# Attention in steps of half a unit: TensorE's work sorted by kinds, eight transposes in two banks, other lags

## The chip, the cores and the metric

The kernel runs on one core of a Trainium2 chip. The metric is the device time of one execution in microseconds (us), as the median of several runs. Five engines work side by side, each on its own queue, in the order of the program: TensorE (PE: matrix products and transposes; its weight loads are listed apart as PEld), VectorE (DVE), ScalarE (ACT), GpSimd (POOL) and SyncE (SP, which issues DMAs). Matrix results land in PSUM, in banks of 512 float32 columns; everything else lives in SBUF.

## The reference

Causal attention for 2 batches of 12 heads, 448 positions and 64 numbers per head, then two feed-forward parts on the 896 tokens, the first with a product of two projections, the second with a SiLU. All inputs are float32.

```
scores = where(mask, -1e9, (q @ k^T) / 8);  attn = softmax(scores);  x = attn @ v
x is laid out as 896 tokens x 768
y = ((x @ w_a) * (x @ w_b)) @ w_out          # w_a, w_b 768 x 1536, w_out 1536 x 768
h = y @ w_in                                 # 768 x 2048
out = (h * sigmoid(h)) @ w2_out              # 2048 x 768
```

## The kernel before

Attention works on 12 units (u) of two heads each; the first six belong to batch 0. The 448 queries of a unit are seven blocks j of 64, and block j meets only the 64*(j+1) keys that the mask leaves. GROUPS deals the blocks out to four slots, so that each slot's scores fill one PSUM bank: (6), (5, 0), (4, 1), (3, 2). One slot of the program holds, in this order on TensorE:

- the scores of a group. A block j >= 3 is multiplied as "halves" (a high and a low part of q and k in a faster float format; three matmuls, L565), a smaller block in plain float32 (one matmul per head, L569). In the trace and in the order's rows these are `sc<-kh,qh` and `sc<-k,q`.
- LAG_PV = 11 slots later the product with v (`xo<-ptr,v`, L627, float32), by blocks of 128 keys: one block in each of a unit's first two slots, two in the third, none in the fourth;
- LAG_T = 5 slots later the transposes of the group's softmax rows (`pt<-ident,p`, L610), four of 128x128 into one PSUM bank. The bank is emptied into `ptr` in SBUF one slot later (L710): by ACT, for block 4 by DVE. There are two such banks, and until slot 32 a third, which is later needed for other work.

Between scores and transposes lies the softmax: DVE adds the mask and takes the extreme of each row (soft, L577), ACT takes the exponential (L581), DVE inverts the rows' sums (normalize, L590 and L591), POOL multiplies the rows by that (L594). Normalize comes twice per unit, each for two groups. POOL also makes the high half of the next unit's q and k (`qh`, `kh`, L538), DVE the low half (`ql`, `kl`, L543). When all four blocks of keys are done, finish copies the unit's result out of PSUM: ACT as `xh` (L383) and `xf` (L385), DVE as `xl` (L389).

The order of the program is written out by the loop over slots: what a slot defers goes to a list (late) with a slot and a priority, and is issued from it in the order of the priorities. Beside attention, the first weights of the dense part are converted from 64-bit words (convert): on DVE L225, L230 and L256, on ACT L213, L219 and L252. A timeline places these, in units of seven matmuls per slot.

Once the scores are through, the loop runs on for the slots in which the lagging transposes and products still come (here called the drain). These are filled with the first products of the dense part, which need batch 0 alone (early_products, `acc`, L295): 12 pieces of three matmuls. Behind the attention come some 450 us of dense products on TensorE.

Of the kernel before, what the change touches and what calls it, by code (L numbers as in the profile page):

```python
# [10 lines left out]
F32 = mybir.dt.float32  # L11
# [19 lines left out]
CONV2 = 52  # L31
WARM = 8
BIG = 3
NQ = 3
SLOT_HI = 0
SLOT_LO = 2
SUMS0 = 44
SUMS_MM = 3
SPARE = 6
# [10 lines left out]
SLOT_MM = 7  # L50
# [12 lines left out]
def fused_kernel(ctx: ExitStack, tc: tile.TileContext, qk, v, w_ab, w_mid, w_in, w_out, out):  # L63
# [33 lines left out]
    ps_g = [ctx.enter_context(tc.tile_pool(name=f"ps_g{i}", bufs=1, space=PSUM)) for i in range(2)]  # L97
# [85 lines left out]
    line = Timeline()  # L183
# [267 lines left out]
    sums_x = Sums()  # L451

    granules = []
# [23 lines left out]
    with tc.manual_schedule():  # L477

        with ExitStack() as actx:
# [6 lines left out]
            sm_p = sctx.enter_context(right(name="sm_p", bufs=3))  # L486
# [24 lines left out]
            nblk = [j // 2 + 1 for j in range(NJ)]  # L511
            p_sb = [[p_p.tile([P, P * nblk[j]], F32, name=f"p{s}_{j}") for j in range(NJ)] for s in range(2)]
            U = [dict() for _ in range(NU)]
            late, now = {}, [0]
            n_slots = NU * len(GROUPS) + LAG_PV + 2
            NS = len(GROUPS)

            def defer(k, prio, fn):
                late.setdefault(now[0] + k, []).append((prio, fn))
# [21 lines left out]
            def halves_lo(u):  # L541
                for n, src, _ in sources(u):
                    nc.vector.tensor_tensor(  # L543
                        out=U[u][n + "l"], in0=src, in1=U[u][n + "h"].bitcast(F32), op=ALU.subtract)

# [1 line left out]
                U[u]["v"] = v_p.tile([P, NKB, P], F32, tag="v", name="v")  # L547
                nc.sync.dma_start(out=U[u]["v"], in_=v[u])

            def scores(u, i):  # L550

                t = U[u]
                if i == 0:
                    for n in ("sums", "nmax", "rcp"):
                        t[n] = st_p.tile([P, NJ], F32, tag=n, name=n)
                bank = ps_s.tile([P, 512], F32, tag="s", name="sc")
                sm = sm_p.tile([P, S], F32, tag="sm", name="sm")
                o = 0
                for j in GROUPS[i]:
                    K = D * (j + 1)  # L560
                    sc = bank[:, o:o + K]
                    o += K
                    if "qh" in t and j >= BIG:
                        for n, (a, k) in enumerate((("qh", "kh"), ("qh", "kl"), ("ql", "kh"))):
                            nc.tensor.matmul(out=sc, lhsT=t[a][:, j - BIG].rearrange("p h q -> p (h q)"), rhs=t[k][:, 0:K],  # L565
                                             start=(n == 0), stop=(n == 2))
                    else:
                        for h in range(2):
                            nc.tensor.matmul(  # L569
                                out=sc[h * D:(h + 1) * D], lhsT=q_sb[u % NQ][:, h, j * D:(j + 1) * D],  # L570
                                rhs=t["k"][:, 0:K], start=True, stop=True,
                            )
                    defer(0, 2, partial(soft, u, j, sc, sm[:, o - K:o], K, COL[j]))

            def soft(u, j, sc, sm, K, c):
                t = U[u]
# [20 lines left out]
                    )  # L597

            def transposes(u, i):
                t = U[u]  # L600
                if i == 0:
                    t["pt"] = pt_p.tile([P, NKB, 2, S], F32, tag="ptr", name="ptr")
                pool, tag = (ps_g[1], "g") if now[0] < b0_done - 4 and now[0] % 3 == 0 else (ps_t, "t")
                bank = pool.tile([P, NKB, 2, D], F32, tag=tag, name="pt")
                o = 0
                for j in GROUPS[i]:
                    pt = bank[:, o:o + nblk[j]]
                    o += nblk[j]
                    for kb in range(nblk[j]):
                        nc.tensor.transpose(  # L610
                            out=pt[:, kb].rearrange("p h q -> p (h q)"),
                            in_=p_sb[u % 2][j][:, kb * P:(kb + 1) * P], identity=ident,
                        )
                    copy = nc.vector.tensor_copy if j in EVAC_DVE else nc.scalar.copy
                    dst = t["pt"][:, 0:nblk[j], :, j * D:(j + 1) * D]
                    defer(1, 1, partial(copy, out=dst, in_=pt))

            def pv(u, kb):
                t = U[u]
                b, chunk = divmod(u, NP)  # L620
                if kb == 0:
                    pool, tag = ps_x, "x"
                    if u % 2:
                        pool, tag = ps_g[0], "g"
                    t["x"] = pool.tile([P, 512], F32, tag=tag, name="xo")
                for h in range(2):
                    nc.tensor.matmul(  # L627
                        out=t["x"][h * D:(h + 1) * D, kb * P:S], lhsT=t["v"][:, kb, h * D:(h + 1) * D],
                        rhs=t["pt"][:, kb, h, kb * P:S], start=(kb == 0), stop=(kb == NKB - 1),
                    )  # L630
                if kb == NKB - 1:
                    defer(1, 0, partial(finish, b, chunk, t["x"][:, 0:S]))

            tasks = []

# [26 lines left out]
            line.now = -n_slots * SLOT_MM  # L662
            line.convert(granules[0], (CONV0 - n_slots) * SLOT_MM, (CONV1 - CONV0) * SLOT_MM)
            line.convert(granules[1], (CONV1 + 1 - n_slots) * SLOT_MM, (CONV2 - CONV1) * SLOT_MM)
# [12 lines left out]
            b0_done = (NP - 1) * NS + LAG_PV + NKB + 1  # L677
            fill, n_fill = early_products(), 2 * NP
            done_fill = 0
            fill0 = NU * NS + 2  # L680
            for s in range(n_slots):
                now[0] = s
                if s == NU * NS + 1:
# [5 lines left out]
                u, i = divmod(s, NS)  # L689
                if i == 0 and 0 < u and u + 2 < NU:  # L690
                    load_qk(u + 2)
                if i == SLOT_HI and u + 1 < NU:
                    halves_hi(u + 1)
                if i == SLOT_LO and u + 1 < NU:
                    halves_lo(u + 1)
                if i == 0 and 0 < u <= NU:
                    load_v(u - 1)
                for what, lag in ORDER:
                    u, i = divmod(s - lag, NS)
                    if not 0 <= u < NU:  # L700
                        continue
                    if what == "scores":
                        scores(u, i)
                    elif what == "transposes":
                        transposes(u, i)
                    else:
                        for kb in PV[i]:
                            pv(u, kb)
                for _, fn in sorted(late.pop(s, ()), key=lambda e: e[0]):
                    fn()  # L710
                while tasks:
                    tasks.pop(0)()
                u, i = divmod(s - LAG_N, NS)
                if 0 <= u < NU and i % 2 == 1:
                    normalize(u, (i - 1, i))
                if s >= SUMS0:
                    sums_x.step()
                line.to((s + 1 - n_slots) * SLOT_MM)
                want = n_fill * max(0, s + 1 - fill0) // (n_slots - 3 - fill0)
                while done_fill < min(want, n_fill):  # L720
                    next(fill, None)
                    done_fill += 1
            run(fill)
            for fn in sorted(late):
                for _, f in late[fn]:
# [250 lines left out]
```

## Time and profile before

| | us |
|---|---|
| median of 3 runs (571.66 to 571.90) | 571.85 |
| the profiled execution, its own time | 571.69 |
| its span in the trace | 569.9 |
| TensorE busy in the span | 559.3 |
| DVE busy | 421.8 |
| ACT busy | 380.5 |
| POOL busy | 72.2 |

The span is what the trace covers; the time of an execution is 1.8 us more. Busy times are sums over the whole span. Attention fills roughly the first 107 us, so its part is read from stretches of that part alone, and a unit in steady state is one stretch that ends where the fourth group's transposes start the next unit.

### The profile page before, as it was taken

To read this page: it belongs to the slowest core of one execution; us is meant where nothing else is said; L and a number is where in the kernel's file an instruction comes from. 1 tells how busy PE (TensorE), PEld (TensorE's weight loads), DVE (VectorE), ACT (ScalarE), POOL (GpSimd) and SP (SyncE) were. 2 spreads that over 40 slices of the span, in tenths; PEclk is the share of its full clock that TensorE was granted. 3 is DMA by queue.
4 is the path that set the end of the run, shared out by engine and by line. 5 is a ranking of instruction groups with operands and counts; after the bars stand their busy time and mean duration, and the time that the engine had idled before them with its cause. 6 is when DMAs were issued, how large, how long until landed. Compare 5 with 4: busy or idle time off the path is not lost.

```text
span 569.9 us, 8400 instructions
## 1 busy us (share of the span) xinstructions
PE 559.3 (98%) x2978; PEld 490.4 (86%) x2978; DVE 421.8 (74%) x794; ACT 380.5 (67%) x754; POOL 72.2 (13%) x127
## 2 busy tenths in 40 slices
PE   8999997999999999999999999999999999999997
PEld 6666664799999999999999999999999999999996
DVE  6798887587989898969875688978887798342500
ACT  4989988674766666668745475888786996532601
POOL 6887764000000000000000000000000000000000
PEclk9999999999999999999999999999999999999999
DMA  7355323032333434333333333333324233541501
GB/s 246 116 178 139 121 65 141 1 112 110 112 110 112 136 134 161 117 118 109 114 110 112 110 112 110 112 113 110 112 96 143 75 113 111 165 142 54 176 0 64
DMA packets 18233, 65.41 MB, mean 115 GB/s; under 512 B 2192, under 2 KB 6928, under 8 KB 18192
## 3 DMA queue, kind: packets, MB, share of 16 engines
q1 hardware_dynamic: 18048, 64.77, 33.6%
q8 instruction: 23, 0.38, 0.3%
q14 instruction: 18, 0.15, 0.1%
q10 hardware_dynamic: 144, 0.11, 0.1%
HBM read 62.13 MB, written 2.75 MB: 114 GB/s over the span
## 4 chain that ended last, share of the span: by engine, by line
PE 93%; DVE 2%; ACT 2%; POOL 1%; issue 1%; DMA 1%; SPq 0%; POOLq 0%; DVEq 0%; ACTq 0%
PE acc L295 82%; PE pt L610 4%; PE xo L627 3%; PE sc L565 3%; PE sc L569 2%; DVE sm L577 1%; POOL p L594 1%; ACT ptr L710 1%; DMA k<-qk 1%; DVE wq L230 0%; ACT xf L385 0%; ACT p L581 0%; ACT xh L383 0%; DVE kl L543 0%; DVE ql L543 0%
## 5 line engine op out<-in xcount | busy, mean ns | idle before, releaser
L225 DVE SCALAR_TENSOR_TENSOR wq<-wr 128x768 uint32<-128x768 uint32 (+1 forms) x76 | 66.5, 877 | 28.4 <-ACT wr L219 27.7
L318 ACT COPY s<-acc 128x448 f32<-128x448 f32 x72 | 38.4, 533 | 63.1 <-PE acc L295 62.7
L219 ACT ACTIVATE wr<-wr,wbias 128x768 uint32<-128x768 uint32 (+1 forms) x76 | 69.9, 920 | 0.0
L213 ACT ACTIVATE wr<-wr 128x768 f32<-128x768 f32 (+1 forms) x76 | 63.8, 840 | 5.4 <-DMA wr<-w_out 4.0
L230 DVE SCALAR_TENSOR_TENSOR wq<-wr,wq 128x768 uint32<-128x768 uint32 (+1 forms) x76 | 64.0, 873 | 0.1
L594 POOL TENSOR_SCALAR p<-p,rcp 128x448 f32<-128x448 f32 (+6 forms) x84 | 56.3, 685 | 21.3 <-ACT p L581 15.6
L581 ACT ACTIVATE p<-sm,nmax 128x448 f32<-128x448 f32 (+6 forms) x84 | 43.0, 523 | 10.5 <-DVE nmax L577 9.5
L295 PE MATMUL acc<-th,wgbl 128*128 128x448 f32 x168 | 49.5, 366 | 0.0
L295 PE MATMUL acc<-th,wgbh 128*128 128x448 f32 x168 | 49.4, 366 | 0.0
L295 PE MATMUL acc<-th,wgal 128*128 128x448 f32 x168 | 49.4, 365 | 0.0
L295 PE MATMUL acc<-tl,wgah 128*128 128x448 f32 x168 | 49.4, 366 | 0.0
L295 PE MATMUL acc<-tl,wgbh 128*128 128x448 f32 x168 | 49.4, 365 | 0.0
L295 PE MATMUL acc<-th,wgah 128*128 128x448 f32 x168 | 49.3, 365 | 0.0
L610 PEld LDWEIGHTS pt<-ident,p 128*128 128x128 f32 x192 | 20.2, 141 | 22.4 <-issue 10.8
L610 PE MATMUL pt<-ident,p 128*128 128x128 f32 x192 | 31.0, 285 | 5.5 <-ACT ptr L710 4.4
L577 DVE CUSTOM_DVE_ANT_0 sm<-sc,mask 128x448 f32<-128x448 f32 (+6 forms) x84 | 31.9, 411 | 4.8 <-PE sc L569 4.8
L295 PEld LDWEIGHTS acc<-th,wgbh 128*128 128x128 f32 x168 | 31.5, 188 | 2.9 <-DVE s L767 0.2
L295 PEld LDWEIGHTS acc<-th,wgah 128*128 128x128 f32 x168 | 31.5, 188 | 2.7
L295 PEld LDWEIGHTS acc<-tl,wgah 128*128 128x128 f32 x168 | 31.6, 188 | 2.6
L295 PEld LDWEIGHTS acc<-th,wgal 128*128 128x128 f32 x168 | 31.5, 188 | 2.5
L295 PEld LDWEIGHTS acc<-th,wgbl 128*128 128x128 f32 x168 | 31.5, 188 | 2.5
L295 PEld LDWEIGHTS acc<-tl,wgbh 128*128 128x128 f32 x168 | 31.5, 188 | 2.5
(167 smaller groups left out, 1384.2 us busy)
## 6 DMA issues: line engine op xcount, KB each, us to landing
wr<-w_ab SPq DMA_DIRECT2D x24, 768.0 KB, 4.9
wr<-w_in SPq DMA_DIRECT2D x16, 768.0 KB, 4.5
wr<-w_out SPq DMA_DIRECT2D x24, 512.0 KB, 4.4
wr<-w_mid SPq DMA_DIRECT2D x12, 768.0 KB, 4.6
v<-v SPq DMA_DIRECT2D x12, 256.0 KB, 4.2
q<-qk SPq DMA_DIRECT2D x24, 112.0 KB, 2.8
k<-qk SPq DMA_DIRECT2D x12, 224.0 KB, 3.3
out<-o SPq DMA_DIRECT2D x11, 224.0 KB, 5.4
```

What stands on the lines that cost most here:

```text
L213: nc.scalar.activation(out=word(i, 1).bitcast(F32), in_=word(i, 1).bitcast(F32), func=AF.Copy, scale=2.0 ** -112)
L219: nc.scalar.activation(out=word(i, 0), in_=word(i, 0), func=AF.Relu, bias=wbias, scale=2.0 ** -29)
L225: nc.vector.scalar_tensor_tensor(out=xi(i), in0=word(i, 1), scalar=3, in1=word(i, 0), op0=ALU.logical_shift_left, op1=ALU.bitwise_or)
L230: nc.vector.scalar_tensor_tensor(out=xi(i), in0=word(i, 1), scalar=0x80000000, in1=xi(i), op0=ALU.bitwise_and, op1=ALU.bitwise_or)
L295: nc.tensor.matmul(out=acc[:, 0:S], lhsT=w, rhs=a, start=first, stop=last, skip_group_check=True)
L318: nc.scalar.copy(out=t, in_=acc[:, 0:S])
L565: nc.tensor.matmul(out=sc, lhsT=t[a][:, j - BIG].rearrange("p h q -> p (h q)"), rhs=t[k][:, 0:K], start=(n == 0), stop=(n == 2))
L577: nc.vector.tensor_tensor_reduce(out=sm, in0=sc, in1=mask[:, S - K:S], op0=ALU.add, op1=ALU.min, scale=-(D ** -0.5), scalar=3.0e38, accum_ ...
L581: nc.scalar.activation(out=p_sb[u % 2][j][:, 0:K], in_=sm, func=AF.Exp, bias=t["nmax"][:, c:c + 1], scale=-1.0, accum_out=t["sums"][:, c:c ...
L594: nc.gpsimd.tensor_scalar(out=pj, in0=pj, scalar1=t["rcp"][:, COL[j]:COL[j] + 1], scalar2=1.0, op0=ALU.mult, op1=ALU.mult,)
L610: nc.tensor.transpose(out=pt[:, kb].rearrange("p h q -> p (h q)"), in_=p_sb[u % 2][j][:, kb * P:(kb + 1) * P], identity=ident,)
L627: nc.tensor.matmul(out=t["x"][h * D:(h + 1) * D, kb * P:S], lhsT=t["v"][:, kb, h * D:(h + 1) * D], rhs=t["pt"][:, kb, h, kb * P:S], start= ...
```

## The change

The loop now counts steps of half a unit, two groups each. In a step TensorE gets first all halves products of both groups, then their float32 scores, then the product with v for two blocks of keys (LAG_PV = 5 steps), then eight transposes (LAG_T = 2 steps). The eight transposes go into two banks, and the table COPIES says which block lies where and who empties it: in a unit's first half one bank by a single ACT copy of 512 columns, the other by three copies on DVE; in the second half one bank by an ACT copy of 512, the other by ACT copies of 384 and 128. For that, most transposes write their 128 columns as two runs of 64. The third bank serves every third bank while u < 8. The deferred work of a step is sorted differently: ACT's copies, then finish, then the low halves and all softs of the step, then DVE's copies and normalize. The 12 early pieces come in four steps from step 24 on, at the start of each.

```diff
-PV = ((0,), (1,), (2, 3), ())
-EVAC_DVE = (4,)
-LAG_N = 1
-LAG_T = 5
-LAG_PV = 11
-ORDER = (("scores", 0), ("pv", LAG_PV), ("transposes", LAG_T))
+COPIES = (
+    ((0, "scalar", 0, 2, 5, 2), (1, "vector", 2, 1, 5, 2), (1, "vector", 3, 1, 6, 1), (1, "vector", 0, 1, 0, 1)),
+    ((0, "scalar", 0, 1, 1, 4), (1, "scalar", 1, 1, 2, 3), (1, "scalar", 2, 1, 4, 1)),
+)
+LAG_T = 2
+LAG_PV = 5
+FILL_STEPS = 4
...
-            def scores(u, i):
+            def scores(u, groups):
...
+                for n, j, sc in sorted(work, key=lambda e: e[1] < BIG):
                     K = D * (j + 1)
...
-                    defer(0, 2, partial(soft, u, j, sc, sm[:, o - K:o], K, COL[j]))
+                if groups[0] and u + 1 < NU:
+                    defer(0, 2, partial(halves_lo, u + 1))
+                for n in range(len(groups)):
+                    defer(0, 2, partial(soft_group, u, [(j, sc) for m, j, sc in work if m == n]))
...
-                pool, tag = (ps_g[1], "g") if now[0] < b0_done - 4 and now[0] % 3 == 0 else (ps_t, "t")
-                bank = pool.tile([P, NKB, 2, D], F32, tag=tag, name="pt")
...
+                bank = []
+                for _ in range(2):
+                    pool, tag = (ps_g[1], "g") if n_banks[0] % 3 == 2 and u < NP + 2 else (ps_t, "t")
+                    n_banks[0] += 1
+                    bank.append(pool.tile([P, 512], F32, tag=tag, name="pt"))
+                place, o = {}, [0, 0]
+                for n, copy, kb, nkb, j, nj in COPIES[i]:
+                    size = nkb * nj * 2 * D
+                    src = bank[n][:, o[n]:o[n] + size].rearrange("p (k h q) -> p k h q", k=nkb, h=2)
...
+                            place[j + c, kb + a] = src[:, a, :, c * D:(c + 1) * D]
...
+                    if copy == "vector":
+                        defer(1, 3, partial(nc.vector.tensor_copy, out=dst, in_=src))
+                    else:
+                        defer(1, 0, partial(nc.scalar.copy, out=dst, in_=src))
...
+            for d in range(n_steps):
...
+                while done_fill < min(n_fill * max(0, d + 1 - 2 * NU) // FILL_STEPS, n_fill):
+                    next(fill, None)
+                    done_fill += 1
+                if u < NU:
+                    scores(u, (2 * i, 2 * i + 1))
+                u, i = divmod(d - LAG_PV, 2)
+                if 0 <= u < NU:
+                    for kb in range(2 * i, min(2 * i + 2, NKB)):
+                        pv(u, kb)
+                u, i = divmod(d - LAG_T, 2)
+                if 0 <= u < NU:
+                    transposes(u, i)
+                u, i = divmod(d - 1, 2)
+                if 0 <= u < NU:
+                    defer(0, 3, partial(normalize, u, (2 * i, 2 * i + 1)))
+                for _, fn in sorted(late.pop(d, ()), key=lambda e: e[0]):
+                    fn()
```

On TensorE, before, the first two slots of a unit in steady state read as follows (a number at a name's end tells q's and p's buffers apart, `x2` is a repeated row):

```order
L565 MATMUL sc<-kh,qh 128x448
L565 MATMUL sc<-kl,qh 128x448
L565 MATMUL sc<-kh,ql 128x448
L627 MATMUL xo<-ptr,v 64x320 x2
L610 MATMUL pt<-ident,p_3_124 128x128 x2
L610 MATMUL pt<-ident,p_2_123 128x128 x2
L565 MATMUL sc<-kh,qh 128x384
L565 MATMUL sc<-kl,qh 128x384
L565 MATMUL sc<-kh,ql 128x384
L569 MATMUL sc<-k,q_118 64x64 x2
L627 MATMUL xo<-ptr,v 64x192 x2
L627 MATMUL xo<-ptr,v 64x64 x2
```

Each slot goes from halves to float32 and on to its own transposes. After the change, the first half of a unit stands on TensorE like this:

```order
L568 MATMUL sc<-kh,qh 128x448
L568 MATMUL sc<-kl,qh 128x448
L568 MATMUL sc<-kh,ql 128x448
L568 MATMUL sc<-kh,qh 128x384
L568 MATMUL sc<-kl,qh 128x384
L568 MATMUL sc<-kh,ql 128x384
L572 MATMUL sc<-k,q_119 64x64 x2
L654 MATMUL xo<-ptr,v 64x192 x2
L654 MATMUL xo<-ptr,v 64x64 x2
L642 MATMUL pt<-ident,p_6_134 128x2x64 x3
L642 MATMUL pt<-ident,p_6_134 128x128
L642 MATMUL pt<-ident,p_5_133 128x2x64 x3
```

Two groups' halves now stand together, then the float32 work, then eight transposes, most with an output of 2x64.

On DVE, before, the last two slots of a unit stand like this (`sm,nmax` is a soft, `ptr<-pt` a bank's copy):

```order
L577 ISA sm,nmax<-sc,mask 128x128
L577 ISA nmax 128x1
L389 TENSOR_TENSOR xl<-xo,xh 128x448
L590 TENSOR_SCALAR sums<-sums 128x3
L591 RECIPROCAL rcp<-sums 128x3
L577 ISA sm,nmax<-sc,mask 128x256
L577 ISA nmax 128x1
L577 ISA sm,nmax<-sc,mask 128x192
L577 ISA nmax 128x1
L710 COPY ptr<-pt 128x6x64
```

The normalize of the first two groups (sums over three columns) comes between the softs of the last two slots. After the change, the second half of a unit stands on DVE like this:

```order
L543 TENSOR_TENSOR kl<-k,kh 128x448
L591 ISA sm,nmax<-sc,mask 128x320
L591 ISA nmax 128x1
L591 ISA sm,nmax<-sc,mask 128x128
L591 ISA nmax 128x1
L591 ISA sm,nmax<-sc,mask 128x256
L591 ISA nmax 128x1
L591 ISA sm,nmax<-sc,mask 128x192
L591 ISA nmax 128x1
L737 COPY ptr<-pt 128x2x128
L737 COPY ptr<-pt 128x2x64 x2
L604 TENSOR_SCALAR sums<-sums 128x3
```

The same normalize now stands behind all four softs of the step and behind three copies where one was.

## Rows read from the trace of the kernel before

**Rows 1.** The page: span, and busy time of each engine.

```profile
span 569.9 us, 8400 instructions
PE 559.3 (98%) x2978; PEld 490.4 (86%) x2978; DVE 421.8 (74%) x794; ACT 380.5 (67%) x754; POOL 72.2 (13%) x127
```

**Rows 2.** Busy time by stretches: a stretch of dense products.

```profile
core 0: us, PE busy (x) PEld busy (x) DVE busy (x) ACT busy (x) POOL busy (x), PEclk, DMA share, GB/s
200.00:300.00 100.00, 100.00 (x492) 92.02 (x491) 85.82 (x127) 68.52 (x107) 0.00 (x0) 1.00 0.35 121
```

**Rows 3.** Busy time by stretches, one for each of three units.

```profile
35.73:43.00 7.27, 7.27 (x60) 4.87 (x58) 7.05 (x28) 6.21 (x23) 6.32 (x11) 1.00 0.69 242
43.00:50.26 7.26, 7.26 (x59) 4.86 (x58) 5.22 (x23) 7.26 (x25) 5.20 (x9) 1.00 0.61 159
...
65.26:73.87 8.61, 7.36 (x60) 4.88 (x58) 5.69 (x23) 8.61 (x27) 5.21 (x9) 1.00 0.36 111
```

**Rows 4.** Chain that ended last, 38 to 64: start, us, what.

```profile
45.91 0.44 PE xo L627 x8
...
47.39 0.37 PE sc L569 x4
47.76 0.59 PE pt L610 x4
```

**Rows 5.** The same chain, 86 to 112, where early products stand ahead.

```profile
106.78 0.59 PE xo L627 x8
```

**Rows 6.** TensorE's timeline, 60 to 98: start, us, what [idle before <-releaser].

```profile
93.55 1.13 PE L610 MATMUL pt<-ident,p 128*128 128x128 f32 x8 [0.95 <-ACT ptr L710]
...
96.64 0.63 PE L610 MATMUL pt<-ident,p 128*128 128x128 f32 x4 [0.47 <-ACT ptr L710]
```

**Rows 7.** Waits, 62 to 108: us in total, times, longest.

```profile
PE pt L610 <- ACT ptr L710: 4.4, 6, 1.4
```

**Rows 8.** ACT by line and shape, 21.20 to 57.53 (five units): busy, mean ns | idle.

```profile
L710 ACT COPY ptr<-pt 128x512 f32<-128x512 f32 x6 | 3.7, 617 | 0.0
...
L710 ACT COPY ptr<-pt 128x256 f32<-128x256 f32 x10 | 3.2, 377 | 0.0
...
L710 ACT COPY ptr<-pt 128x128 f32<-128x128 f32 x10 | 2.9, 288 | 0.9 <-DVE ptr L710 0.9
```

**Rows 9.** DVE by line and shape, the same five units.

```profile
L710 DVE COPY ptr<-pt 128x384 f32<-128x384 f32 x5 | 2.7, 548 | 0.0
...
L230 DVE SCALAR_TENSOR_TENSOR wq<-wr,wq 128x768 uint32<-128x768 uint32 x2 | 2.2, 1098 | 0.0
...
L577 DVE CUSTOM_DVE_ANT_0 sm<-sc,mask 128x256 f32<-128x256 f32 x5 | 2.0, 394 | 0.0
L577 DVE CUSTOM_DVE_ANT_0 sm<-sc,mask 128x192 f32<-128x192 f32 x5 | 1.8, 352 | 0.0
L577 DVE CUSTOM_DVE_ANT_0 sm<-sc,mask 128x128 f32<-128x128 f32 x5 | 1.4, 279 | 0.0
```

**Rows 10.** Timeline of all engines, 40 to 52, the path from normalize to the next soft.

```profile
43.21 0.16 DVE L590 TENSOR_SCALAR sums<-sums 128x3 f32<-128x3 f32 x1
43.41 0.18 DVE L591 RECIPROCAL rcp<-sums 128x3 f32<-128x3 f32 x1
43.75 1.49 POOL L594 TENSOR_SCALAR p<-p,rcp 128x448 f32<-128x448 f32 x3 [0.83 <-ACT p L581]
45.20 0.62 POOL L538 TENSOR_SCALAR qh<-q 128x512 fp32r<-128x512 f32 x1
45.79 0.56 POOL L538 TENSOR_SCALAR kh<-k 128x448 fp32r<-128x448 f32 x1
47.33 0.61 DVE L543 TENSOR_TENSOR kl<-k,kh 128x448 fp32r<-128x448 f32 x1
47.86 0.48 DVE L577 CUSTOM_DVE_ANT_0 sm<-sc,mask 128x320 f32<-128x320 f32 x1
```

**Rows 11.** POOL's timeline, 60 to 108: the same three multiplications, later.

```profile
82.42 2.19 POOL L594 TENSOR_SCALAR p<-p,rcp 128x448 f32<-128x448 f32 x3 [1.32 <-ACT p L581]
```

More of the change, by code (lines that the diff above doesn't have):

```diff
@@ L548, in load_v @@
                 nc.sync.dma_start(out=U[u]["v"], in_=v[u])
-            def scores(u, i):
+            def scores(u, groups):
                 t = U[u]
-                if i == 0:
+                if groups[0] == 0:
                     for n in ("sums", "nmax", "rcp"):
                         t[n] = st_p.tile([P, NJ], F32, tag=n, name=n)
[L556 to L559, printed above, removed]
+                work = []
+                for n, i in enumerate(groups):
+                    bank = ps_s.tile([P, 512], F32, tag="s", name="sc")
+                    o = 0
+                    for j in GROUPS[i]:
+                        work.append((n, j, bank[:, o:o + D * (j + 1)]))
+                        o += D * (j + 1)
+                for n, j, sc in sorted(work, key=lambda e: e[1] < BIG):
                     K = D * (j + 1)
-                    sc = bank[:, o:o + K]
-                    o += K
                     if "qh" in t and j >= BIG:
-                        for n, (a, k) in enumerate((("qh", "kh"), ("qh", "kl"), ("ql", "kh"))):
+                        for i, (a, k) in enumerate((("qh", "kh"), ("qh", "kl"), ("ql", "kh"))):
                             nc.tensor.matmul(out=sc, lhsT=t[a][:, j - BIG].rearrange("p h q -> p (h q)"), rhs=t[k][:, 0:K],
-                                             start=(n == 0), stop=(n == 2))
+                                             start=(i == 0), stop=(i == 2))
                     else:
@@ L572, in scores, with soft_group @@
                             )
-                    defer(0, 2, partial(soft, u, j, sc, sm[:, o - K:o], K, COL[j]))
+                if groups[0] and u + 1 < NU:
+                    defer(0, 2, partial(halves_lo, u + 1))
+                for n in range(len(groups)):
+                    defer(0, 2, partial(soft_group, u, [(j, sc) for m, j, sc in work if m == n]))
+            def soft_group(u, chunks):
+                sm = sm_p.tile([P, S], F32, tag="sm", name="sm")
+                o = 0
+                for j, sc in chunks:
+                    K = D * (j + 1)
+                    soft(u, j, sc, sm[:, o:o + K], K, COL[j])
+                    o += K
             def soft(u, j, sc, sm, K, c):
@@ L602, in transposes @@
                     t["pt"] = pt_p.tile([P, NKB, 2, S], F32, tag="ptr", name="ptr")
-                pool, tag = (ps_g[1], "g") if now[0] < b0_done - 4 and now[0] % 3 == 0 else (ps_t, "t")
-                bank = pool.tile([P, NKB, 2, D], F32, tag=tag, name="pt")
[L605 to L616, printed above, removed]
+                bank = []
[7 more added lines that the diff above has]
+                    src = bank[n][:, o[n]:o[n] + size].rearrange("p (k h q) -> p k h q", k=nkb, h=2)
+                    o[n] += size
+                    dst = t["pt"][:, kb:kb + nkb, :, j * D:(j + nj) * D]
+                    for a in range(nkb):
+                        for c in range(nj):
+                            place[j + c, kb + a] = src[:, a, :, c * D:(c + 1) * D]
+                    if nkb == 1:
+                        src, dst = src[:, 0], dst[:, 0]
+                    if copy == "vector":
+                        defer(1, 3, partial(nc.vector.tensor_copy, out=dst, in_=src))
+                    else:
+                        defer(1, 0, partial(nc.scalar.copy, out=dst, in_=src))
+                for g in (2 * i, 2 * i + 1):
+                    for j in GROUPS[g]:
+                        for kb in range(nblk[j]):
+                            nc.tensor.transpose(
+                                out=place[j, kb], in_=p_sb[u % 2][j][:, kb * P:(kb + 1) * P], identity=ident)
             def pv(u, kb):
@@ L661, in fused_kernel @@
             load_ahead()
[L662 to L664 removed]
+            line.now = -2 * n_steps * SLOT_MM
+            line.convert(granules[0], (CONV0 - 2 * n_steps) * SLOT_MM, (CONV1 - CONV0) * SLOT_MM)
+            line.convert(granules[1], (CONV1 + 1 - 2 * n_steps) * SLOT_MM, (CONV2 - CONV1) * SLOT_MM)
             first = []
@@ L675, in early_products @@
                         yield
[L677 to L683, printed above, removed]
+            fill, n_fill, done_fill = early_products(), 2 * NP, 0
+            for d in range(n_steps):
+                now[0] = d
+                u, i = divmod(d, 2)
+                if u == NU and i == 0:
                     sctx.close()
@@ L688, in fused_kernel @@
                     banks.add(ctx.enter_context(right(name="ps_r", bufs=3, space=PSUM, reuse_waits="tile")), 3)
-                u, i = divmod(s, NS)
                 if i == 0 and 0 < u and u + 2 < NU:
                     load_qk(u + 2)
-                if i == SLOT_HI and u + 1 < NU:
+                if i == 0 and u + 1 < NU:
                     halves_hi(u + 1)
-                if i == SLOT_LO and u + 1 < NU:
-                    halves_lo(u + 1)
                 if i == 0 and 0 < u <= NU:
                     load_v(u - 1)
[L698 to L709, printed above, removed]
+                while done_fill < min(n_fill * max(0, d + 1 - 2 * NU) // FILL_STEPS, n_fill):
[14 more added lines that the diff above has]
+                for _, fn in sorted(late.pop(d, ()), key=lambda e: e[0]):
                     fn()
@@ L712, in fused_kernel @@
                     tasks.pop(0)()
[L713 to L722, printed above, removed]
+                for n in range(2):
+                    if 2 * d + n >= SUMS0:
+                        sums_x.step()
+                    line.to((2 * d + n + 1 - 2 * n_steps) * SLOT_MM)
             run(fill)
```

8 lines of the change are left out of this document (3 added, 5 removed).

## The prediction

> **What bounds the kernel now.** I read the page first. TensorE is busy 559.3 of the 569.9 us of the span, DVE 421.8, ACT 380.5 [rows 1]. So the reader looks at TensorE first, and at the others only where TensorE waits for them. The second view is the busy time by stretches. Behind attention TensorE is busy 100.00 of 100.00 us, DVE 85.82 [rows 2]. A gain in attention therefore reaches the end, as long as the weights that DVE and ACT prepare come as early as now.
>
> Within attention the same view goes by units. In steady state TensorE is busy 7.27 of 7.27 us: it is the bound there, though DVE is busy 7.05 in one such unit and ACT 7.26 of 7.26 in the next [rows 3]. In a later unit ACT is busy 8.61 of 8.61 and TensorE only 7.36 of it [rows 3]. The waits name it: from 62 us on TensorE's transposes wait 4.4 us in six pieces for ACT's copies [rows 7]. Steady units thus have little slack beside TensorE, and late units have none.
>
> **What sorting saves on TensorE.** The chain of waits lists TensorE's work piece by piece. The product with v of 192 and 64 columns (eight matmuls) takes 0.44 right behind float32 scores [rows 4] and 0.59 right behind halves products [rows 5]. So going from halves to float32 costs 0.59 - 0.44 = 0.15. Two slots make this passage twice, a step once: 0.15 saved per step.
>
> Four transposes behind float32 take 0.59 [rows 4]. Eight in a row take 1.13 and four take 0.63, both after an idle [rows 6], so a further four cost 0.50, and 0.09 is saved where two blocks of four become one. The upper bound is the 0.15 of the other passage; I take 0.12, between the two, since leaving the transposes for halves happens once less too. A unit of two steps saves 2 x (0.15 + 0.12) = 0.54 (bounds 0.48 and 0.60) and would take 7.27 - 0.54 = 6.73. Scores run for 24 steps and the product with v lags by five, so 19 steps, some nine units, hold all three kinds: **-4.9** (bounds -4.3 and -5.4).
>
> In the drain the order has eight slots with products with v behind halves and five with transposes; after, four and two. That is 4 x 0.15 + 3 x 0.12: **-1.0** (bounds -0.6 without the transposes, -1.1 with 0.15 for all seven).
>
> **What it costs on the other engines.** ACT's copies per unit lose two of 256 columns and one of 128 (2 x 0.377 + 0.288) and gain one of 512 (0.617) [rows 8]: -0.42. DVE had one copy of 384 at 0.548 and gets three, of 256, 128 and 128. The trace has no DVE copy of that size; I take the softs of those sizes, which also read PSUM, 0.394 + 2 x 0.279 = 0.95 [rows 9]: +0.40 per unit. That costs nothing where DVE has room: 5.22 + 0.40 is below 6.73 [rows 3]. With two weight conversions of 1.098 [rows 9] in a unit it does not: 7.05 + 0.40 = 7.45 [rows 3], 0.72 over 6.73. The timeline that places the conversions puts two into each of two units among the first ones. The neighbours have 1.1 of slack each, so half may be taken up: **+0.7** (bounds 0 and +1.4).
>
> At the start, the first transposes wait for normalize, which now stands behind two more softs, 0.394 + 0.352 [rows 9]: **+0.5** (bounds 0 and +0.75). Later in the program the lag of two steps covers this.
>
> **The late units.** In the unit that ACT filled, ACT would need 8.61 - 0.42 = 8.19, so it still sets the pace, and gains 0.42 where I counted 0.54. Behind that unit ACT's relief of 0.42 per unit goes against what is left of the 4.4 us of waits [rows 7]. Against it stands that the eight transposes need both banks: with two banks left (from unit 8 on, eight steps) both must have been emptied in the same step. If each of the eight steps waited the present mean of 4.4 / 6 = 0.73, that would be 5.9, 1.5 more than now; if only the two waits behind the last scores stay, 0.95 + 0.47 [rows 6], it is 3.0 less. I take **-0.8** (bounds -3.0 and +1.5), because ACT's copies now come first of all in a step.
>
> The sum: -4.9 - 1.0 + 0.7 + 0.5 - 0.8 = -5.5. Against the profiled execution's own 571.69 that gives **566.2**; the median of the runs lies only 0.16 above that execution. The bounds add up to 562.2 (-5.4 - 1.1 + 0 + 0 - 3.0) and to 570.4 (-4.3 - 0.6 + 1.4 + 0.75 + 1.5).
>
> **The rivals.** A measurement of this kernel tells about 0.2%, 1.1 us, from no change.
>
> First, a ring of DVE and POOL binds before TensorE does. Normalize of the first half stands behind all softs and copies of its step, POOL's multiplications come next, then the next high halves, then DVE's low halves, then the softs and copies, then normalize again. Its length from rows: sums 0.16 + 0.18, POOL 1.49, high halves 0.62 + 0.56, low half 0.61 [rows 10], softs of the four blocks 0.48 [rows 10] + 0.28 + 0.39 + 0.35, copies 0.95 [rows 9]: 6.07. That is under 6.73, so it doesn't bind by itself. It does when POOL takes 2.19 for the same work, as it did once [rows 11] (6.77), or when one conversion of 1.098 falls into it (7.17). If most units went at 7.17, nine would save 9 x 0.10 = 0.9 instead of 4.9, and the 0.7 is in that already: 571.69 - 0.9 - 1.0 + 0.5 - 0.8 = 569.5.
>
> Second, and on the other side: the banks. A step needs two banks. DVE's copies of one of them stand behind all softs of the step, and these behind the low halves. TensorE reaches the transposes after its scores and the product with v. If DVE's softs, 1.50 as above, end after TensorE has got there, the copies' 0.95 lie on TensorE's path. For: ACT's copies are already what the transposes wait for [rows 7]. Against: with three banks a step before unit 8 needs only one bank of the step just before, and that is the one which ACT empties first. At the present mean wait of 0.73 in every second step, 11 times, it costs 8.0: 571.69 - 5.5 + 8.0 = 574.2. It decides from 5.5 / 11 = 0.50 per unit.
>
> Third, also on the other side: the transposes' new output. Thirteen of sixteen per unit write two runs of 64 instead of one of 128. No row of before has such an output. A transpose inside a block costs 0.50 / 4 = 0.125 [rows 6]; if it took twice that, 12 x 13 x 0.125 = 19.5 would come on top: 571.69 - 5.5 + 19.5 = 585.7. It decides from 5.5 / 156 = 0.035 per transpose. Against: each run is still 64 columns long, so there is one break per 128 columns. The Trainium skill's page "PSUM — Partial Sum Buffer", section "Specifications (TRN2)", speaks against the change here: it says that any non-contiguous access pattern slows matmuls significantly. No run here shows yet whether a break every 64 columns counts as one; by that rule this rival would hold.
>
> Fourth, the change does not do what it says: the 0.15 is no passage between kinds but belongs to the product with v when the early products stand ahead of it. Then nothing but the start is left: 571.69 + 0.5 = 572.2. Against it stands that two different pieces, products and transposes, show the same sign [rows 4 to 6].
>
> **How the numbers follow.** Forecast 0.60; the ring 0.19; the banks 0.11; the output's runs 0.05; nothing saved 0.05. The ring gets most because its cover is 0.66 us wide and conversions are longer. The range from 562.2 to 571.6 holds the forecast's bounds, the ring and half of the cases without a gain; the banks and the runs, 0.16, and some of the last case stay out. Faster by over 0.2% (under 570.6): the forecast and most of the ring, 0.75. Within 0.2%: what is left of the ring, and the last case, 0.09. Slower: the banks and the runs, 0.16.
>
> **What the profile after would show.** Right: steady units of about 6.73 with TensorE busy throughout; one passage to float32 per step in the chain; eight transposes at about 1.1; DVE's copies at about 0.95 per unit, ACT's copies 0.42 less. The ring: TensorE idle before transposes for POOL's `p`, and units of about 7.2. The banks: TensorE idle before transposes for DVE's `ptr`, above all from unit 8 on. The runs: a row for the 2x64 transposes with a higher mean than the contiguous ones. What would make the prediction wrong most easily is a wait on DVE's in-order queue, where a conversion, low halves, softs, copies and normalize now follow each other without the gaps that four slots gave.

## The result and the profile after

The changed kernel takes 566.69 us (median of 4 runs, 566.35 to 567.45) where the kernel before took 571.88 in the same comparison: a ratio of 0.9911 (95% interval 0.9894 to 0.9928). The forecast was 566.2. The slowest of the four runs is the one whose mean granted clock of TensorE was 0.997; the other three, at 1.00, took 566.35 to 566.70. The profiled execution of the changed kernel took 566.35, so the two profiles differ by 571.69 - 566.35 = 5.3 us.

The page of the changed kernel, which answers to [rows 1]:

```profile
span 564.5 us, 8382 instructions
PE 553.8 (98%) x2978; PEld 493.7 (87%) x2978; DVE 426.6 (76%) x818; ACT 376.7 (67%) x730; POOL 72.8 (13%) x127
```

TensorE's busy time falls by 5.5 us and its idle time stays (10.6 before, 10.7 after). To see where, I cut both traces at the same places of the program: the start of unit 3's scores, the end of the last scores, and the end of attention together with all 36 early matmuls. The view is busy time by stretches: stretch, its length, then PE, PEld, DVE, ACT and POOL. First the kernel before, then the changed one:

```profile
0.00:21.20 21.20, 18.97 (x125) 13.71 (x125) 14.02 (x60) 14.03 (x44) 15.32 (x41) 1.00 0.68 211
21.20:89.95 68.75, 65.30 (x503) 43.41 (x502) 57.78 (x206) 63.74 (x210) 51.72 (x79) 1.00 0.44 137
89.95:108.58 18.63, 17.10 (x104) 11.23 (x105) 11.90 (x28) 11.76 (x33) 5.20 (x7) 1.00 0.06 25
```

```profile
0.00:23.24 23.24, 20.12 (x133) 14.64 (x133) 16.17 (x68) 15.32 (x47) 15.58 (x42) 1.00 0.64 201
23.24:89.68 66.44, 62.23 (x507) 46.24 (x505) 60.98 (x226) 60.09 (x191) 52.22 (x80) 1.00 0.44 140
89.68:103.97 14.29, 14.29 (x96) 10.69 (x94) 11.16 (x21) 9.31 (x24) 5.03 (x7) 1.00 0.06 25
```

Attention ends 4.6 us earlier. The start is 2.0 longer, the nine units 2.3 shorter, the drain 4.3 shorter. The lags are shorter by half a step, so one block of four transposes and one product with v, about 1.2 us of TensorE's work, moves from the drain to the start; without that the start is 0.8 longer and the drain 3.1 shorter. The missing 0.75 us lies in the dense products, whose program the change does not touch. Rows of the chain show it (start, duration, count): the kernel before, that kernel with a third bank (the last experiment below), and the changed one:

```profile
107.37 459.13 PE acc L295 x2256
```

```profile
106.27 459.09 PE acc L295 x2256
```

```profile
103.97 457.16 PE acc L295 x2250
```

A dense matmul took 459.13 / 2256 = 0.2035 before and 457.16 / 2250 = 0.2032 after. The difference goes with the kernel and not with the execution: both traces of the old order show 459.1, and all eleven of the changed kernel and its variants 457.11 to 457.20. It lies in the first dense product: from the first to the 40th copy of a result into `s` (L318) the kernel before takes 123.37 us (132.57 to 255.94) and the changed one 122.58 (128.03 to 250.61). Why, no run here shows.

Now the single units after the change:

```profile
23.24:30.17 6.93, 6.89 (x59) 5.12 (x57) 5.69 (x22) 6.93 (x24) 5.56 (x9) 1.00 0.27 88
30.17:37.61 7.44, 7.31 (x60) 5.13 (x58) 7.37 (x25) 5.72 (x19) 6.62 (x9) 1.00 0.47 157
37.61:44.85 7.24, 6.88 (x58) 5.09 (x58) 7.17 (x28) 6.22 (x23) 5.92 (x9) 1.00 0.57 190
...
51.53:58.20 6.67, 6.67 (x60) 5.14 (x58) 6.60 (x26) 6.67 (x26) 5.93 (x9) 1.00 0.36 110
...
64.86:73.28 8.42, 7.16 (x59) 5.14 (x58) 6.42 (x28) 8.42 (x26) 5.62 (x10) 1.00 0.36 104
73.28:82.42 9.14, 7.10 (x59) 5.16 (x58) 8.88 (x29) 7.36 (x28) 7.32 (x10) 1.00 0.28 86
```

An undisturbed unit takes 6.67 (7.27 before [rows 3]). Two early units are longer because DVE is nearly full in them (7.37 of 7.44), one late unit because ACT is full (8.42 of 8.42), the next because DVE is (8.88 of 9.14). Nine undisturbed units would take 60.0 us, and the nine took 66.44: 6.4 us went to waits. (TensorE is listed as idle for 66.44 - 62.23 = 4.2 of them; short waits inside a block of transposes count as busy.) Before it was 68.75 - 9 x 7.27 = 3.3. So the sorting gave 9 x 0.60 = 5.4 in these units and the waits took 3.1 of it back.

The chain of the changed kernel shows one step and the next one's first work without an idle:

```profile
26.62 0.79 PE sc L568 x6
27.41 0.69 PE sc L572 x8
28.10 1.29 PE xo L654 x8
29.39 1.02 PE pt L642 x8
30.41 0.62 PE sc L568 x3
```

Eight transposes take 1.02 where two blocks of four took 1.18 [rows 4]. In the two early units with conversions the chain leaves TensorE, and the transposes wait for POOL's multiplied rows:

```profile
34.04 2.93 POOL p L608 x3
37.01 0.84 PE pt L642 x4
...
39.30 1.29 POOL p L608
40.64 0.66 PE pt L642 x4
```

What DVE does ahead of the worst wait is seen in the timeline of the long unit (start, duration, engine and line):

```profile
76.41 0.93 DVE L225 SCALAR_TENSOR_TENSOR wq<-wr 128x768 uint32<-128x768 uint32 x1
77.25 0.95 DVE L230 SCALAR_TENSOR_TENSOR wq<-wr,wq 128x768 uint32<-128x768 uint32 x1
...
80.76 0.81 DVE L737 COPY ptr<-pt 128x256 f32<-128x256 f32 x3
...
81.71 0.95 PE L642 MATMUL pt<-ident,p 128*128 128x128 f32 x7 [2.01 <-DVE sums L604]
```

Two conversions stand ahead of the low halves and softs, DVE's three copies behind them. The transposes start when these copies end, 2.01 us late; the row names the instruction on DVE that comes next. So does the view of waits from 62 us on (us in total, times, longest), where ACT's share has fallen from 4.4 [rows 7] to 1.1:

```profile
PE pt L642 <- DVE sums L604: 2.4, 2, 2.0
...
PE pt L642 <- ACT ptr L737: 1.1, 2, 0.9
```

### The profile page after: what moved, and what is told of

Its sections match the earlier page's. It is cut to its first block, busy times and chain, and to the rows that moved or that the text cites. A ratio compares the mean times of both kernels' runs of the same rounds, so it can differ in the third digit from the quotient of the medians.

```text
span 564.5 us, 8382 instructions
## 1 busy us (share of the span) xinstructions
PE 553.8 (98%) x2978; PEld 493.7 (87%) x2978; DVE 426.6 (76%) x818; ACT 376.7 (67%) x730; POOL 72.8 (13%) x127
## 4 chain that ended last, share of the span: by engine, by line
PE 89%; DVE 5%; issue 2%; POOL 2%; ACT 1%; DMA 1%; SPq 0%; DVEq 0%; ACTq 0%; POOLq 0%
PE acc L295 82%; PE pt L642 2%; DVE sm L591 2%; PE sc L568 2%; POOL p L608 2%; PE xo L654 1%; PE sc L572 1%; DVE ptr L737 1%; DVE kl L543 1%; DMA k<-qk 1%; ACT p L595 0%; DVE sums L604 0%; ACT ptr L737 0%; SPq L526 0%; DVE wgal L256 0%
## 5 line engine op out<-in xcount | busy, mean ns | idle before, releaser
L318 ACT COPY s<-acc 128x448 f32<-128x448 f32 x72 | 38.5, 534 | 61.0 <-PE acc L295 60.6
L642 PE MATMUL pt<-ident,p 128*128 128x128 f32 x192 | 29.2, 284 | 6.0 <-DVE sums L604 2.4
L256 DVE TENSOR_TENSOR wgal<-wq,wgah 128x512 fp32r<-128x512 f32 (+1 forms) x20 | 16.4, 820 | 23.2 <-ACT wgah L252 14.3
```

The costliest lines, as they stand in the source:

```text
L256: nc.vector.tensor_tensor(out=view[1], in0=src(), in1=view[0].bitcast(F32), op=ALU.subtract)
L318: nc.scalar.copy(out=t, in_=acc[:, 0:S])
L642: nc.tensor.transpose(out=place[j, kb], in_=p_sb[u % 2][j][:, kb * P:(kb + 1) * P], identity=ident)
```

## The experiments

### One more passage from halves to float32 per step

TensorE's order in a step becomes halves, float32, halves, float32, transposes; nothing else is changed.

```diff
...
-                for n, j, sc in sorted(work, key=lambda e: e[1] < BIG):
...
+                for w, (n, j, sc) in enumerate(work):
+                    if w and work[w - 1][0] != n and between:
+                        pv(*between.pop(0))
...
```

> The changed kernel, but TensorE's order in a step is: scores of one group, half of the product with v, scores of the other group, the other half, then the eight transposes. That is one more passage from halves to float32 per step; lags, banks, copies and the other engines' orders stay. Theory (the passages are what was saved): each of some 20 steps pays 0.15 us again, steady units go from 6.67 to 6.97 or a little more, and the time is 569 to 570. Rival (the gain is from shorter lags and from ACT's fewer copies): units stay at 6.67 and the time at 566.7.

572.23 us against 571.81 for the kernel before (ratio 1.0005, 0.9996 to 1.0015): the whole gain is gone. A steady unit in the view of stretches, and this kernel's chain:

```profile
53.82:61.18 7.36, 7.36 (x59) 4.89 (x58) 6.83 (x26) 6.30 (x23) 5.91 (x9) 1.00 0.34 100
```

```profile
53.04 1.02 PE pt L647 x8
54.07 0.61 PE sc L571 x3
54.68 0.48 PE xo L659 x4
55.16 0.72 PE sc L571 x3
```

The theory is confirmed in kind, and its price was too low, for a passage goes both ways. The second group's three halves products take 0.72 behind the product with v; behind other halves they take 1.13 - 0.61 = 0.52 (six take 1.13 in the next experiment's chain). So the way back from float32 to halves costs 0.20 on top of 0.15 for the way there, 0.35 per step or 0.69 per unit.

### Two blocks of four transposes per step

Half of the product with v comes between the two blocks.

```diff
...
                 for g in (2 * i, 2 * i + 1):
+                    if g % 2:
+                        for a in between:
+                            pv(*a)
                     for j in GROUPS[g]:
...
```

> The changed kernel, but the eight transposes of a step stand in two blocks of four with half of the product with v between them; all else stays. Theory: a second block costs 0.12 us per step, so steady units take 6.9 and the time is about 568.7. Rival (a block of eight is worth nothing, since transposes and products with v are both float32): units stay at 6.67 and the time at 566.7.

571.57 us (ratio 1.0000, 0.9991 to 1.0010): this alone gives the gain back too. A steady unit and the chain:

```profile
46.64:53.90 7.26, 7.26 (x59) 4.92 (x58) 6.37 (x26) 7.26 (x24) 5.24 (x10) 1.00 0.56 163
```

```profile
51.53 0.75 PE xo L657 x4
52.29 0.59 PE pt L645 x4
52.87 0.69 PE xo L657 x4
53.56 0.59 PE pt L645 x4
54.15 1.13 PE sc L568 x6
```

Transposes are a kind of their own. Two blocks take 1.18 where eight in a row take 1.02, and the two halves of the product 1.44 where together they take 1.29. Going to transposes costs 0.16 and coming back to float32 0.15: 0.31 per step, and steady units are at 7.26, where they were before the change [rows 3]. Only from transposes to halves is nothing paid: three halves products of 448 columns behind transposes take 0.61 or 0.62, as three dense ones do (3 x 0.2032).

By this price list the old order (halves, float32, transposes, twice) pays 2 x (0.15 + 0.16) = 0.62 per two slots and the new one 0.31 per step: 0.62 per unit, and 0.60 is measured. Neither experiment is the old order in steps: the first also adds a way back from float32 to halves, which the old order did not have.

### The banks' old layout and copies

Each transpose writes one run of 128 columns again, each group has its own bank, and ACT copies all blocks but block 4.

```diff
-                for n, copy, kb, nkb, j, nj in COPIES[i]:
...
+                for n in range(2):
+                    o = 0
+                    for j in GROUPS[2 * i + n]:
+                        src = bank[n][:, o:o + nblk[j] * P].rearrange("p (k h q) -> p k h q", k=nblk[j], h=2)
+                        o += nblk[j] * P
...
+                        if j == 4:
+                            defer(1, 3, partial(nc.vector.tensor_copy, out=dst, in_=src))
+                        else:
+                            defer(1, 0, partial(nc.scalar.copy, out=dst, in_=src))
```

> The changed kernel with the banks' old layout: each transpose writes one run of 128 columns, each group has its own bank, ACT copies block by block, DVE block 4 alone. Theory (two runs of 64 cost TensorE nothing; the new copies move 0.4 us per unit from ACT to DVE): blocks of eight transposes and steady units stay at 6.67, the two units with two DVE conversions get up to 0.4 shorter, the unit that ACT fills 0.4 longer; the time is 566 to 567.5. Rival (the two runs slow the transposes): steady units fall below 6.6 and the time under 565.

566.90 us (ratio 0.9913, 0.9898 to 0.9927), as the changed kernel. One row of its chain and one of TensorE's timeline:

```profile
58.71 1.02 PE pt L640 x8
```

```profile
41.28 0.63 PE L640 MATMUL pt<-ident,p 128*128 128x128 f32 x4 [0.61 <-DVE ptr L735]
```

Eight transposes with one run each take the same 1.02, so the two runs of 64 cost nothing, and the rival falls. The Trainium skill's page "PSUM — Partial Sum Buffer", section "Specifications (TRN2)", says that any non-contiguous pattern slows matmuls significantly; in these runs a break every 64 columns does not slow the float32 transposes. The other half of the expectation failed: the early units got no shorter, since TensorE now waits between the two blocks of four for a bank that hangs on DVE's one copy of block 4. The new table of copies is worth nothing measurable by itself.

### The third bank for all units

```diff
-                    pool, tag = (ps_g[1], "g") if n_banks[0] % 3 == 2 and u < NP + 2 else (ps_t, "t")
+                    pool, tag = (ps_g[1], "g") if n_banks[0] % 3 == 2 else (ps_t, "t")
```

> The changed kernel with the third bank kept for all units instead of u < 8. Theory (the late waits of 0.9, 0.2, 2.0 and 0.4 us before transposes are for banks that ACT and DVE empty late): most of 3.5 us go, the time is 563.5 to 564.5. Rival (DVE's and POOL's queues are late themselves, and the waits move to POOL's multiplied rows or to the next step): 566 to 566.7.

564.69 us (ratio 0.9872, 0.9858 to 0.9887): 2.0 less than the changed kernel. The two late units:

```profile
64.66:72.59 7.93, 7.11 (x60) 5.15 (x58) 5.99 (x27) 7.93 (x24) 5.67 (x10) 1.00 0.34 110
72.59:80.07 7.48, 7.35 (x59) 5.12 (x58) 7.36 (x23) 6.61 (x24) 6.82 (x9) 1.00 0.20 59
```

The unit with DVE's conversions falls from 9.14 to 7.48, the one that ACT fills from 8.42 to 7.93. The first is mostly a wait for a bank, and that goes; the second is ACT's own time, and mostly stays.

### DVE's copies ahead of the softs

```diff
-                        defer(1, 3, partial(nc.vector.tensor_copy, out=dst, in_=src))
+                        defer(1, 1.5, partial(nc.vector.tensor_copy, out=dst, in_=src))
```

> The changed kernel with DVE's copies of a bank ahead of the step's low halves and softs instead of behind them. Theory (the late waits of 2.0 and 0.4 us are for the bank that DVE empties behind conversions and softs): these waits go, the softs of every second step come 0.8 us later but under cover of 6.67 us units, and the time is 564.3 to 565.3. Rival (what is short there is DVE's time, not the order): the softs' delay turns into waits for POOL's multiplied rows and the time stays at 566 to 567.5.

565.39 us (ratio 0.9888, 0.9874 to 0.9903), 1.3 less than the changed kernel and just above the range of the theory. The waits for DVE's bank are gone, but unit 3 starts at 24.55 instead of 23.24, as the first softs wait.

### The second conversion spread, without and with the third bank

The same work of the second weights' conversion, from slot 28 on instead of 35.

```diff
-            line.convert(granules[1], (CONV1 + 1 - 2 * n_steps) * SLOT_MM, (CONV2 - CONV1) * SLOT_MM)
+            line.convert(granules[1], (28 - 2 * n_steps) * SLOT_MM, 24 * SLOT_MM)
```

> The changed kernel with the second weights' conversion spread over slots 28 to 52 instead of 35 to 52, so that no unit has three of DVE's conversions; the same work in all. Theory (the long units of 8.42 and 9.14 us are made by conversions that stand in DVE's and ACT's queues ahead of softs and exponentials): both fall to about 7.2 and the time to 563 to 564.5. Rival (the load only moves): earlier units grow from 6.67 to 7.5 or more and the time is 566 or above.

568.03 us (ratio 0.9929, 0.9915 to 0.9944), 1.3 more than the changed kernel. Three of the four runs, with a mean granted clock of 0.997, took 568.02 to 568.05, the fourth, with 0.999, 567.04.

> The changed kernel with both: the third bank for all units and the conversion spread over slots 28 to 52. Theory (bank and conversion are two conditions of the same waits): less than the sum of the two alone, 562.5 to 564. Rival (two separate losses): the gains add up, below 562.5.

566.02 us (ratio 0.9890, 0.9873 to 0.9906), 1.3 more than with the third bank alone. Again three runs (565.92 to 566.13) had a clock of 0.996 or 0.997, and the fourth, at 1.00, took 564.55, as with the third bank alone (564.69). Both theories failed: the load moved into one earlier unit, where it cost what it saved, and most of the 1.3 goes with the clock. The order of the program tells why. Conversions are taken from one list, and the second one's first steps come only when the first one's last is out; so ACT's four steps fell into one step of the loop, ahead of ACT's copies. The stretches of that unit, without the third bank:

```profile
60.50:62.58 2.08, 0.09 (x2) 0.00 (x1) 2.05 (x8) 2.08 (x4) 2.08 (x4) 0.95 0.00 0
62.58:64.50 1.92, 1.92 (x9) 1.92 (x10) 1.38 (x2) 1.92 (x9) 1.92 (x3) 0.50 0.00 0
64.50:66.40 1.90, 1.90 (x15) 1.58 (x16) 0.30 (x1) 1.48 (x5) 0.56 (x2) 0.66 0.00 0
```

TensorE was busy 0.09 of 2.08 us, and then ran at a granted clock of 0.50, its lower level (1.2 GHz, against 2.4 at 1.00), so a wait of 2.0 cost more than 2.0.

### Transposes ahead of the float32 work

The order in a step is halves, transposes, float32, with the third bank for all units.

```diff
...
+                done = not between
                 for n, j, sc in sorted(work, key=lambda e: e[1] < BIG):
+                    if j < BIG and not done:
+                        done = True
+                        between[0]()
...
```

> The version with the third bank for all units, and within a step the order halves, transposes, float32 instead of halves, float32, transposes: the same number of passages, but other ones. Theory (each passage has its own price; in the two runs with more passages float32 to halves cost about 0.20, transposes to float32 0.15, transposes to halves nothing): a step pays 0.35 plus whatever halves to transposes costs, instead of 0.30, so steady units take 6.77 to 7.1. Rival (only the number of passages counts): 6.67.

608.43 us in one run, 42 more than the changed kernel, and neither theory's number: units take about 10 us. Two of the longest pieces of its chain, and a unit with a stretch in which the clock fell:

```profile
56.15 1.29 POOL p L612
59.77 2.12 POOL p L612 x3
```

```profile
44.72:54.51 9.79, 7.82 (x58) 5.26 (x56) 6.67 (x22) 4.93 (x16) 6.46 (x9) 1.00 0.42 142
...
101.00:103.00 2.00, 0.33 (x1) 0.14 (x1) 0.31 (x1) 2.00 (x4) 1.84 (x4) 0.82 0.24 92
103.00:108.60 5.60, 5.55 (x24) 3.06 (x24) 3.05 (x15) 3.38 (x12) 0.48 (x1) 0.50 0.00 0
```

The float32 scores now stand behind transposes that wait for POOL. Their softs, and with them the next sums and POOL's next multiplications, wait in turn. This is a ring like that of the first rival, but closed through TensorE: POOL, transposes, scores, softs, normalize, POOL. The unit shown takes 9.79 at a clock of 1.00, so the clock is only a part of the loss. The run says nothing on the price of the passage that it was made for.

### Conversions placed evenly, with the third bank

Both conversions get due times that keep DVE's steps apart and start the second only when the first is out.

```diff
...
+            granules[0]["due"] = dict(join=(0.15, 0.32), sign=(0.49, 0.62), ghi=(0.64, 0.72), glo=(0.80, 0.92))
+            granules[1]["due"] = dict(exp=(0.0, 0.14), low=(0.07, 0.21), join=(0.28, 0.40), sign=(0.52, 0.64),
+                                      ghi=(0.74, 0.82), glo=(0.88, 1.0))
...
+            line.convert(granules[0], (8 - 2 * n_steps) * SLOT_MM, 26 * SLOT_MM)
+            line.convert(granules[1], (32 - 2 * n_steps) * SLOT_MM, 20 * SLOT_MM)
```

> The changed kernel with the third bank for all units, and both weights' conversions placed so that each unit has at most one or two of DVE's steps and ACT's four do not stand together. Theory (the long units 4 and 5 at 7.4 and 7.2 us, and what is left of units 9 and 10, come from two or three conversions in one unit's queue): units 4 and 5 fall to 6.7 to 6.9, units 9 and 10 to about 7, and the time to 562 to 563.3. Rival (the load only moves, as when the second conversion alone was spread): other units grow and the time stays at 564.3 or above.

563.21 us (ratio 0.9858, 0.9841 to 0.9876), within the theory's range and 3.5 below the changed kernel; 2.0 of that is the third bank's, 1.5 the placement's. The nine units, and two of them:

```profile
23.38:86.29 62.91, 61.93 (x507) 46.12 (x506) 59.91 (x223) 59.07 (x189) 51.41 (x79) 1.00 0.40 126
```

```profile
30.32:36.99 6.67, 6.67 (x59) 5.14 (x58) 5.96 (x22) 5.79 (x20) 5.76 (x9) 1.00 0.35 112
36.99:44.14 7.15, 7.07 (x60) 5.11 (x58) 7.08 (x26) 5.84 (x21) 5.90 (x9) 1.00 0.48 158
```

Of the 6.4 us of waits in the nine units 2.9 are left. The unit that had taken 7.44 now takes 6.67, but its neighbour still 7.15 with DVE busy 7.08 of it: part of the load only moved. In that unit too the chain goes through POOL's rows: its multiplications from 40.58 to 43.50 hold back the last transposes, which follow at 43.54.

With DVE's copies first as well:

> The same with DVE's copies ahead of the step's low halves and softs as well. Theory (with three banks nobody waits for DVE's bank any more, so its copies may stand last): no gain, 0 to 0.8 us slower than without, since softs and normalize come later at the start. Rival (order on DVE still matters with three banks): 0.5 us or more faster.

563.16 us (ratio 0.9848, 0.9834 to 0.9862): no difference, as the theory said.

### The kernel before with the third bank

```diff
-                pool, tag = (ps_g[1], "g") if now[0] < b0_done - 4 and now[0] % 3 == 0 else (ps_t, "t")
+                pool, tag = (ps_g[1], "g") if now[0] % 3 == 0 else (ps_t, "t")
```

> The kernel before with the third bank kept for all slots; nothing else of the change. Theory (its late waits of 4.4 us are for ACT, which is full there, and a bank only moves a wait): 571 to 572. Rival (a third bank lifts late waits in either kernel alike): 569.5 to 570.3, as it took 2.0 off the changed kernel.

571.42 us (ratio 0.9996, 0.9987 to 1.0005): no difference. In the old order a slot needs one bank at a time. In this trace the waits for ACT's copies fall from 4.4 [rows 7] to 2.2, but TensorE now waits 1.2 for DVE's low half and 0.6 for POOL's rows: the late waits are for engines that are full. The need for the third bank came with the change.

## Why the prediction was right, and where it was not

The total was right, and in part by luck: four terms were too small in size, one gain did not come, a gain that has no term in the sum did, and these errors cancelled.

| term | predicted | measured |
|---|---|---|
| sorting, nine units | -4.9 | 9 x 0.60 = -5.4 |
| passages in the drain | -1.0 | 17.10 - 14.29 busy, less the 1.2 that moved: -1.6 |
| start | +0.5 | 23.24 - 21.20, less the 1.2 that moved: +0.8 |
| early units with conversions | +0.7 | 6.93 + 7.44 + 7.24 - 3 x 6.67 = +1.6 |
| late units and waits in the drain | -0.8 | (6.4 - 1.6) - (3.3 + 1.5) = 0.0 |
| attention | -5.5 | -4.6 |
| pace of the dense products | 0 | -0.75 |

The sorting: right in kind, shown by two experiments that each put one kind of passage back, whereupon the time is that of the kernel before. The mis-sized term is the second passage. I took 0.12 for it, between 0.09 and 0.15; it is 0.16, just above the upper bound. The two rows of transposes that gave 0.09 came behind an idle: eight took 1.13, 0.11 more than the 1.02 of a block without one, and four 0.63, only 0.04 more than 0.59. The reason I gave for going above 0.09, that leaving the transposes costs something too, is wrong for the halves that follow them.

The drain: the count was wrong, and the way back from float32 was left out. The trace of before has six products with v behind early pieces, not eight, against four after. By the price list that is 2 x 0.15, with 3 x 0.16 for three blocks of transposes less, 2 x 0.15 for two ways from transposes to the product with v, and 2 x 0.20 for two ways from the product with v back to early pieces: 1.48 of the 1.6.

The other engines: the new DVE copies measure 0.414 + 2 x 0.276 = 0.97 against 0.95, and ACT's copies take 0.50 less per unit against 0.42. DVE's two forms in the changed kernel, over six units:

```profile
L737 DVE COPY ptr<-pt 128x128 f32<-128x128 f32 x12 | 2.8, 276 | 0.0
L737 DVE COPY ptr<-pt 128x256 f32<-128x256 f32 x6 | 2.5, 414 | 0.0
```

What failed is the step from DVE's sum to the unit. I let the neighbours take up half of the excess. The excess is not only a sum: a conversion also delays what is queued behind it, POOL's work among it, and nothing was taken up. This is the first rival, the ring, under the condition that it named, a conversion within it. From one normalize of a first half to the next (L604, sums over three columns, at 22.49, 30.21, 38.16 and 44.97) two rounds with conversions took 7.72 and 7.95 and the next 6.81. TensorE fell behind with them: in the units of 7.44 and 7.24 it waited for POOL's rows.

The late units: the relief of ACT did take the 1.5 us of idle out of the drain, but the units ahead gave it back. Here the second rival was partly true, at the place that it named: with two banks, DVE's copies behind conversions and softs lay on TensorE's path, 2.0 and 0.4 us. The third bank removes 2.0 us, and moving the copies ahead of the softs 1.3. It did not decide, since in early units three banks and 6.67 us gave cover. The first rival, the ring, did not bind in most units, as its price of 569.5 needed: the unit shown and its two neighbours ran at 6.67 without an idle.

The third rival is excluded by the old layout, the fourth by the first two experiments. The 0.75 us of the dense products come with the changed kernel in every trace, and the prediction has no term for them; without them the profiled execution would have taken 567.1, still inside the range.

Open stay the cause of the 0.75 us, and how much of the start's 0.8 is the order of normalize. That the first weights' conversion still costs 0.5 us per unit when it is spread fits the ring with one conversion: the prediction had 7.17, the unit of 7.15 lies between normalizes 7.22 apart (37.47 and 44.69), and its chain goes through POOL's rows. No run takes this ring apart.

## What to carry to other kernels

Where TensorE is the bound, list its work by kinds in the order of the program and price each passage from rows: here 0.15 to 0.20 us each, and only transposes to halves free. Sorting by kinds pays until a queue elsewhere is asked for more at one time, so look next at what the bigger blocks need at once (here two banks) and at what stands ahead of it on the engine that frees it. A term of slack must be read for the order within a queue, not for the sum over a unit.

## What was not expected of the hardware

A wait of some two microseconds can cost more than itself. In the profiled run with the spread conversion TensorE was busy 0.09 of 2.08 us, and the granted clock was 0.50 in the next stretch of 1.92 and 0.66 in the one behind it; six transposes took 1.54 there. In the changed kernel a wait of 2.01 us at 79.70, with a transpose of 0.33 ahead of it, left the clock at 1.00. Nor is it the program alone: with the third bank as well, three of the four runs had a mean clock of 0.996 or 0.997 and took 565.92 to 566.13, and the fourth had 1.00 and took 564.55. What decides, these runs do not tell.
